# Four F blocks computed ahead instead of six, in a linear-attention and gated-FFN kernel

## The chip, the cores and the metric

The kernel runs on one core of one Trainium2 chip. TensorE (PE) multiplies matrices, VectorE (DVE), ScalarE (ACT) and GpSimd (POOL) work on elements, and SyncE (SP) issues most of the transfers. Each engine takes its own instructions strictly in the order in which they were written out; between engines only semaphores order the work. The metric is the device time of one execution in microseconds, as the median of several runs.

## The reference

```python
def reference(A_x, A_wqkv, A_w_phi, A_wo, B_x, B_w_gate, B_w_up, B_w_down):
    xn = _layernorm(A_x)
    # attention: q, k, v from xn @ wqkv, 32 heads of 18
    pq = einsum("bhsd,hdf->bhsf", q, w_phi); pk = the same of k
    phi = concatenate([softmax(p), softmax(-p)])        # of pq and of pk
    kv = einsum("bhsf,bhsd->bhfd", phi_k, v); z = phi_k.sum(s)
    s = (phi_q @ kv / (phi_q . z + 1e-6)).reshape(B, S, D) @ wo
    # gated feed-forward
    b = (silu(xn @ w_gate) * (xn @ w_up)) @ w_down
    return A_x + s * silu(b)
```

There are 2048 rows and 576 columns. The feed-forward has F = 4608 inner columns, which the kernel cuts into 36 blocks of 128: the F blocks 0 to 35.

## The kernel before

Every fp32 operand of a product is split into a high and a low part, and a product is the sum of three matmuls of parts, so that the result is accurate to fp32. The program has four sections that follow each other: the first loads and normalises x and folds the weights (until about 60 us), the second makes keys, values and their sums (to about 230 us), the third makes the queries, the attention output and its projection (to about 490 us; `q_tile`, `numer` and `project`), and the fourth is the F section, first for the half i = 0 of the rows, then for i = 1.

In the F section a unit is one F block for one half of the rows. `gate_up` computes the gate and the up product of a unit by Strassen's scheme: seven products of seven matmuls of 512 columns each, 49 in all (line 706), in the PSUM tiles `px`, `py` and `pw`. Its weights come from `gate_up_weights`, one block ahead. For i = 0 they are loaded raw into `ld` (L675), POOL forms four sums and differences (L693 to L696, the two tiles `ld` and `ts`), ACT and DVE make the high and low parts `w` (L58 and L59, the helper `split`), and SP stores them to `w_dram` (L686); for i = 1 they are loaded back from there. The products with w_down (L805, `pd`) are queued in steps of two or four units and are put between the products of the units by `fill`.

Within a unit, the order on ACT matters for what follows: L747 copies `px` to `py` after the first product, L751 and L761 apply silu, and L735 (`snap`) copies `px` out after the products with S2 and S3, on which the next product into `px` waits. On DVE, L740 adds to a snap, and L766 forms the second half of the unit's output, `ha`. L889 on POOL is the first step of the down products of an F pair: it subtracts the two halves of a unit's output.

The first EARLY blocks are not computed there. `early_weights` and `early_tile` compute them in plain form, two products of 14 matmuls of 512 columns for each of two column halves of each i: 56 matmuls for a block and a half of the rows (L92, tile `pe`). Their result goes to DRAM (`h_dram`, L123), and in the F section `stored` reads it back (L722) in place of `gate_up`. Two blocks are begun during the first sections; the others are offered to the scheduler as work of lower priority during the third section, where the scheduler puts them between the matmuls of the queries. The block EARLY - 1 is written last, just ahead of the F section, and the loads of the sums of x that Strassen needs (`operands`, L662) stand between its two halves, since they overwrite x of the half i = 1:

```python
parts = early_weights(EARLY - 1)
early_tile(EARLY - 1, 1, parts)
xo = operands(0)
early_tile(EARLY - 1, 0, parts)
ready = [gate_up_weights(*todo.pop(0))]
```

In the order of the units the early blocks stand at every fourth place, from the second place on for i = 0 and from the first on for i = 1:

```python
for f in range(EARLY):
    order.insert(4 * f + 1 - i, f)
```

At the end of the third section `project` leaves its result in PSUM, ACT copies it out to `so` (L618, two buffers) and issues the store to `s_dram` (L619). The F section's PSUM tiles take the banks of those tiles.

Of the kernel before, what the change touches and what calls it, by code (L numbers as in the profile page):

```python
# [26 lines left out]
GROUPS = [(g * GW, min(GW, D - g * GW)) for g in range((D + GW - 1) // GW)]  # L27
NG = len(GROUPS)
QS = 256
EARLY = 6  # L30
TAILS = (NF - EARLY + 3) // 4
LAG = 3
RUSH = NF - 5
# [13 lines left out]
def gated_hedgehog_kernel(ctx: ExitStack, tc, x, w_qk, w_v, w_phi, wo, w_gu, w_tail, w_down, ident_in, mask_in, out):  # L47
# [22 lines left out]
    s_dram = dram.tile([S, D], F32, name="s_dram")  # L70
    h_dram = dram.tile([2, EARLY, P, HS], F32, name="h_dram")
    x_dram = dram.tile([2, 4, P, 4, P], F32, name="x_dram")
    sum_dram = dram.tile([2, P, 4, 4, 5, P], F32, name="sum_dram")
    w_dram = dram.tile([NF - EARLY, P, 7, 4, P], F32, name="w_dram")
    t_dram = dram.tile([TAILS, 4, 3, 32, 7, P], F32, name="t_dram")
# [24 lines left out]
    def early_weights(f, behind=None):  # L100
        parts = []
        for m in (0, 2):
            raw = epool.tile([P, 2, 3, P], F32, name="raw", bufs=2)
            hi = epool.tile([P, 2, 3, P], F32R, name="wh", bufs=3)
            lo = epool.tile([P, 2, 2, P], F32R, name="wl", bufs=3)
            nc.sync.dma_start(raw, w_gu[f, :, m:m + 2])
            with tc.issue_after(behind.ins) if behind else ExitStack():
                with tc.high_priority():
                    split_rows(hi, lo, raw)
            parts.append((hi, lo))  # L110
        return parts
# [14 lines left out]
    with ExitStack() as att:  # L126
# [510 lines left out]

        for f, halves in [(1, (0,)), (0, (0,))] + [(f, (1, 0)) for f in range(2, EARLY - 1)]:
            parts = first_weights.pop() if f == 1 else early_weights(f, read[2 * NT + 1] if f == 0 else None)
# [28 lines left out]
    def gate_up_weights(i, f):  # L668

        parts, wt = {}, fw.tile([96, 7, P], F32R, name="wt", bufs=2)  # L670
        n, q = divmod(f - EARLY, 4)
        if i == 0:
# [5 lines left out]
        def ready(m, src):  # L678
            k = 1 if m == 6 else 2
            w = fw.tile([P, k, 4, P], F32R, name=f"w{k}", bufs=2 if k == 1 else 4)  # L680
            if i:
                nc.sync.dma_start(w.bitcast(F32), w_dram[f - EARLY, :, m:m + k])
            else:
# [393 lines left out]
```

## Time and profile before

| what | us |
|---|---|
| median of 3 runs | 1647.44 (1646.44 to 1647.74) |
| the profiled execution | 1646.56 |
| its span, first to last instruction | 1644.8 |
| PE busy / DVE busy / ACT busy / POOL busy | 1610.8 / 1171.6 / 719.8 / 652.2 |

The span is followed by the page; what lies outside it in the profiled execution is 1.76 us. Times in the rows are microseconds from the start of the span. A row of the timeline has the start, the length, the engine, the line, the operation, the tiles as output<-input, shapes, a count, and in brackets the idle time before it with what ended it. The chain rows have the start, the length, the engine, the tile, the line and a count. A row of the windows has, for each engine, the busy time and in brackets the number of instructions, and then the granted clock of PE (1.00 is full), the busy share of the DMA engines and GB/s.

### The profile page before, as it was taken

The page shows a single profiled execution, that of the slowest core. Times are in us where ns is not written, and L with a number is a line of the kernel's source. Part 1 is how long each engine was busy: PE and PEld are TensorE (multiplying, and loading weights), DVE is VectorE, ACT ScalarE, POOL GpSimd, SP SyncE. Part 2 cuts the span into 40 slices and gives each one's busy share as a digit, 9 for nine tenths or more (in the row PEclk, how much of TensorE's full clock was granted, in tenths as well). Part 3 has the DMA queues.
Part 4 walks back from the last instruction along what each step waited for, and adds up shares of the span by engine and source line. Part 5 has one row for each costly group of instructions (what it writes and reads, how often), then busy time and mean ns, then how long its engine had stood idle before and what let it go on. Part 6 is the DMA issues. An engine that isn't in the chain of part 4 may idle for free.

```text
span 1644.8 us, 25236 instructions
## 1 busy us (share of the span) xinstructions
PE 1610.8 (98%) x9399; PEld 1432.9 (87%) x9399; DVE 1171.6 (71%) x1729; ACT 719.8 (44%) x1399; POOL 652.2 (40%) x695
## 2 busy tenths in 40 slices
PE   6999999999999999999999999999999999999998
PEld 5899987999988788888888888888888888888887
DVE  7677768989861476887787778845566677666578
ACT  5533344454441365444444444445433333333334
POOL 3485661433210353653555454412333244133132
PEclk9999999999999999999999999999999999999999
DMA  9622243433236545545454545395545556555434
GB/s 281 208 79 78 87 132 116 119 109 119 79 121 218 199 172 179 176 172 179 174 173 172 183 166 179 131 362 164 162 128 162 168 171 213 162 179 184 140 114 173
DMA packets 121276, 266.46 MB, mean 162 GB/s; under 512 B 12770, under 2 KB 52834, under 8 KB 119362
## 3 DMA queue, kind: packets, MB, share of 16 engines
q1 hardware_dynamic: 106188, 244.49, 44.5%
q0 software_dynamic: 3072, 11.02, 2.5%
q10 hardware_dynamic: 11894, 9.35, 1.8%
q8 instruction: 74, 1.21, 0.3%
q14 instruction: 48, 0.39, 0.1%
HBM read 165.98 MB, written 98.83 MB: 161 GB/s over the span
## 4 chain that ended last, share of the span: by engine, by line
PE 91%; DVE 3%; DMA 2%; POOL 1%; issue 1%; ACT 1%; SPq 0%; ACTq 0%; POOLq 0%; DVEq 0%
PE pd L805 24%; PE px L706 24%; PE pw L706 12%; PE p L92 6%; PE pe L92 6%; PE py L706 6%; PE p L614 4%; PE po L594 2%; PE kvp L295 2%; PE vx L383 1%; PE pt L588 1%; PE vw L383 1%; DMA s_dram<-so 1%; PE tp L221 1%; DMA xn<-in_A_x 1%
## 5 line engine op out<-in xcount | busy, mean ns | idle before, releaser
L805 PEld LDWEIGHTS pd<-dw,hh 128*128 128x128 f32 x3048 | 433.0, 189 | 25.1 <-DVE dw L59 2.0
L805 PE MATMUL pd<-dw,hh 128*128 128x288 f32 x3048 | 448.8, 297 | 3.2 <-DVE dw L59 1.5
L706 PE MATMUL px<-X,w 128*128 128x512 f32 x1440 | 373.1, 393 | 1.5 <-ACT w L58 1.0
L706 PEld LDWEIGHTS px<-X,w 128*128 128x128 f32 x1440 | 261.4, 188 | 52.5 <-ACT s L735 3.3
L706 PE MATMUL pw<-X,w 128*128 128x512 f32 x720 | 185.7, 393 | 0.0
L706 PEld LDWEIGHTS pw<-X,w 128*128 128x128 f32 x720 | 134.7, 189 | 30.4 <-DVE s L740 0.3
L740 DVE TENSOR_TENSOR s<-pw,s 128x512 f32<-128x512 f32 x120 | 82.5, 688 | 98.1 <-ACT s L735 87.3
L930 DVE TENSOR_TENSOR acc<-pd,acc 128x576 f32<-128x576 f32 x128 | 96.3, 753 | 78.8 <-PE pd L805 78.7
L92 PE MATMUL pe<-X,wh 128*128 128x512 f32 (+1 forms) x460 | 145.4, 399 | 4.9 <-DVE h L122 2.0
L735 ACT COPY s<-px 128x512 f32<-128x512 f32 x120 | 70.3, 586 | 154.9 <-PE px L706 154.8
L59 DVE TENSOR_TENSOR hh<-ha,hh 128x512 fp32r<-128x512 f32 x140 | 112.5, 829 | 16.9 <-ACT hh L58 15.6
L58 ACT CAST hh<-ha 128x512 fp32r<-128x512 f32 x140 | 82.7, 619 | 95.5 <-PE pd L805 74.4
L902 POOL TENSOR_TENSOR hb<-hb 128x512 f32<-128x512 f32 x34 | 46.3, 1363 | 163.4 <-DVE hb L762 162.8
L92 PEld LDWEIGHTS pe<-X,wh 128*128 128x128 f32 (+1 forms) x460 | 84.9, 189 | 24.0 <-ACT h L119 3.0
L59 DVE TENSOR_TENSOR w<-ld,w 128x512 fp32r<-128x512 f32 (+1 forms) x90 | 76.4, 850 | 34.0 <-ACT w L58 32.9
L706 PE MATMUL px<-X,wt 96*128 96x512 f32 x240 | 94.8, 395 | 0.0
L706 PE MATMUL py<-X,w 128*128 128x512 f32 x360 | 94.4, 396 | 0.1
L915 POOL TENSOR_TENSOR ha<-ha 128x512 f32<-128x512 f32 x34 | 52.6, 1562 | 104.6 <-DVE hh L59 104.6
L889 POOL TENSOR_TENSOR h<-ha,hb 128x512 f32<-128x512 f32 x34 | 44.7, 1314 | 106.5 <-DVE ha L766 66.6
L58 ACT CAST w<-ld 128x512 fp32r<-128x512 f32 (+1 forms) x90 | 49.3, 549 | 82.9 <-POOL ld L696 52.5
L747 ACT COPY py<-px 128x512 f32<-128x512 f32 x60 | 34.3, 572 | 98.1 <-PE px L706 76.9
L693 POOL TENSOR_TENSOR ts<-ld 128x256 f32<-128x256 f32 x30 | 27.8, 927 | 120.6 <-issue 70.8
(262 smaller groups left out, 3254.3 us busy)
## 6 DMA issues: line engine op xcount, KB each, us to landing
w_dram<-w SPq DMA_DIRECT2D x87, 512.0 KB, 2.9
w<-w_dram SPq DMA_DIRECT2D x87, 512.0 KB, 4.3
wt<-t_dram SPq DMA_DIRECT2D x59, 336.0 KB, 3.7
ld<-in_B_w_gu SPq DMA_DIRECT2D x30, 512.0 KB, 4.4
X<-sum_dram SPq DMA_DIRECT2D x8, 1280.0 KB, 9.8
rt<-in_B_w_down SPq DMA_DIRECT2D x33, 288.0 KB, 3.1
rb<-in_B_w_down SPq DMA_DIRECT2D x33, 288.0 KB, 4.4
w_dram<-w SPq DMA_DIRECT2D x29, 256.0 KB, 2.0
```

The lines of the kernel that those rows point to most:

```text
L58: nc.scalar.copy(hi, src)
L59: nc.vector.tensor_sub(lo, src, hi)
L92: last = nc.tensor.matmul(ps, l, r, start=n == 0, stop=n == len(pairs) - 1)
L614: nc.tensor.matmul(ps[:, 0:HALF], a[0:w, g, jc], bw[0:w, g, n], start=k == 0, stop=k == 3 * NG - 1)
L706: nc.tensor.matmul(ps, l, r, start=first and n == 0, stop=last and n == len(mm) - 1, skip_group_check=True)
L735: nc.scalar.copy(t, ps)
L740: nc.vector.tensor_add(t, ps, t)
L805: nc.tensor.matmul(ps, l, r, start=first and n == 0 and m == 0, stop=n == len(hs) - 1 and m == 2, skip_group_check=True)
L889: sub(s, g["h"][0][0], g["h"][0][1])
L902: nc.gpsimd.tensor_add(a21, a21, g["h"][1][1])
L915: sub(a12, a12, g["h"][0][0])
L930: nc.vector.tensor_add(a2, pd[:, :, 0:HALF], a2)
```

## The change

The number of blocks that are computed ahead goes from six to four. Blocks 4 and 5 are then ordinary units of the F section, for both halves of the rows, and two places in each half's order that held a stored block hold one that is computed there.

```diff
-EARLY = 6
+EARLY = 4
```

Three things follow from it. In the third section the early blocks that are offered as filling work are 0 and 1 (in part) and 2, and the block written last is block 3 instead of 5. The arrays `w_dram`, `h_dram` and `in_B_w_tail` have two more, or two fewer, blocks; the number of tail groups stays at 8. And the scheduler writes the engines' instructions in another order. The names of tiles in the rows below carry numbers, which differ between the two programs; the last number counts the tiles.

On PE, at the end of the third section, the last rows of `project` were followed by early blocks. Before:

```order
L614 MATMUL p_4601<-WOH,ol 128x288
L92 MATMUL pe<-X_65,wh 128x512
L92 MATMUL pe<-X_65,wl 128x512
L92 MATMUL pe<-X_65,wh 128x512 x2
L92 MATMUL pe<-X_64,wh 128x512
```

Now the F section follows at once:

```order
L614 MATMUL p_4601<-WOH,ol 128x288
L744 MATMUL py<-X_60,w_5230 128x512
L706 MATMUL px<-X_60,w_5230 128x512 x6
L706 MATMUL px<-X_60,wt 128x512
L706 MATMUL pw<-X_5150,w_5239 128x512 x6
L706 MATMUL pw<-X_5150,wt 128x512
L706 MATMUL py<-X_61,w_5230 128x512 x6
```

In the program before, 214 matmuls of early blocks stand between those two rows, L614 and L744, and now none. In the third section ahead of them (from the last row of L295 to the last of L614) there were 318, and now there are 308; up to the end of the seventh of its eight projections both have 294.

On ACT at the same place, the copies of `project`, the first weights and the first copy of the F section, L747. Before:

```order
L618 COPY so_4617<-p2_4601 128x288
L58 CAST w2_5563<-ld_5560 128x2x256
L119 ACTIVATE h_5237<-pe_5221 128x512
L619 DMA s_dram_68<-so_4617 128x288
L58 CAST w1_5580<-ld_5560 128x256
L119 ACTIVATE h_5271<-pe_5255 128x512
```

Now, with the first unit and the beginning of the second Strassen unit:

```order
L618 COPY so_4617<-p2_4601 128x288
L58 CAST w2_5263<-ld_5260 128x2x256
L619 DMA s_dram_68<-so_4617 128x288
L58 CAST w1_5280<-ld_5260 128x256
L747 COPY py_5285<-px_5284 128x512
...
L58 CAST w1_5375<-ld_5355 128x256
L58 CAST w2_5367<-ts_5357 128x2x256
L751 ACTIVATE py_5380<-py_5380 128x512
L58 CAST w2_5371<-ld_5355 128x2x256
L735 COPY s_5414<-px_5379 128x512
```

L747 of the first unit now stands directly behind the casts of the second set of weights (`ld_5260`), and the first L735 of the second unit behind those of the third set (`ld_5355`).

On POOL, the sums for the third set of weights and the first steps of the down products. Before:

```order
L693 TENSOR_TENSOR ts_5657<-ld_5655 128x256
L895 TENSOR_TENSOR rt_5745<-rt_5745 128x288
L694 TENSOR_TENSOR ts_5657<-ld_5655,ts_5657 128x256
L695 TENSOR_TENSOR ld_5655<-ld_5655 128x256
L896 TENSOR_TENSOR td_5749<-rb_5747,rt_5745 128x288
L696 TENSOR_TENSOR ld_5655<-ld_5655,ts_5657 128x256
L889 TENSOR_TENSOR h_5807<-ha_5587,hb_5588 128x512
L902 TENSOR_TENSOR hb_5588<-hb_5588,hb_5651 128x512
```

Now:

```order
L889 TENSOR_TENSOR h_5507<-ha_5287,hb_5288 128x512
L693 TENSOR_TENSOR ts_5357<-ld_5355 128x256
L694 TENSOR_TENSOR ts_5357<-ld_5355,ts_5357 128x256
L695 TENSOR_TENSOR ld_5355<-ld_5355 128x256
L902 TENSOR_TENSOR hb_5288<-hb_5288,hb_5351 128x512
L696 TENSOR_TENSOR ld_5355<-ld_5355,ts_5357 128x256
```

The four operations on the third set stood ahead of L889 and L902, and now L889 stands ahead of all four and L902 ahead of the last.

## The prediction

> **What bounds the kernel now.** I read the page first, then the busy times in stretches, then the chain that ended last, and last the timeline at the two ends of the stretch that the change removes.
>
> ```profile
> PE 1610.8 (98%) x9399; PEld 1432.9 (87%) x9399; DVE 1171.6 (71%) x1729; ACT 719.8 (44%) x1399; POOL 652.2 (40%) x695
> ```
>
> TensorE (PE) is busy for 98% of the span, so a microsecond of PE work taken away or added is a microsecond of time, unless PE then waits. Whether it waits is a question of the stage:
>
> ```profile
> 300.00:350.00 50.00, 50.00 (x349) 46.06 (x348) 45.98 (x71) 21.22 (x40) 18.36 (x36) 1.00 0.36 105
> 500.00:550.00 50.00, 50.00 (x215) 40.09 (x214) 8.56 (x12) 9.03 (x17) 7.29 (x9) 1.00 0.58 209
> 550.00:600.00 50.00, 46.80 (x219) 37.89 (x219) 32.52 (x44) 25.79 (x51) 23.89 (x23) 0.97 0.55 193
> ```
>
> In the query section (first row; the columns after the length are PE, weight loads, DVE, ACT and POOL) PE has no gap, but DVE is busy for 46 of 50 us: without filling work that section would be DVE's. In the second row only PE has work: these are the early blocks that no gap of the query section had room for. In the third row, the opening of the F section, PE loses 3.2 of 50 us and its granted clock falls to 0.97.
>
> **What is removed.** The early blocks behind the attention's last matmul, and the first matmul of the F section:
>
> ```profile
> 487.96 0.29 PE L614 MATMUL p<-WOH,ol 72*128 72x288 f32 x1
> ...
> 538.98 0.40 PE L744 MATMUL py<-X,w 128*128 128x512 f32 x1
> ```
>
> ```profile
> 493.05 46.09 PE pe L92 x196
> ```
>
> The change takes two blocks, 2 x 2 x 56 = 224 matmuls of 512 columns, out of the early work. The chain row gives 46.09 / 196 = 0.2352 us for one, so 52.7 us of PE. By the order of the instructions almost all of it comes from this stretch: the 214 matmuls between the two rows go, and the query section loses 10 of 318, all in its last eighth. So the cover of the softmax stays, and I cost it at nothing up to there. Of the ten I count four as standing where PE has something else at hand and the rest as standing in waits that will now show; I take 0.3 us of gain, between 0 and 2.35 (all ten).
>
> **What is added.** Two Strassen units for each half of the rows. The price is in the chain, as the distance between the same place in two groups of four units, first with one stored block in the group, then with none:
>
> ```profile
> 714.06 4.80 PE pd L805 x36
> ...
> 770.44 4.80 PE pd L805 x36
> ...
> 912.18 4.19 PE px L706 x18
> ...
> 980.02 4.20 PE px L706 x18
> ...
> 1297.77 4.98 PE pd L805 x36
> ...
> 1354.31 4.98 PE pd L805 x36
> ...
> 1457.56 4.19 PE px L706 x18
> ...
> 1525.42 4.19 PE px L706 x18
> ```
>
> For i = 0 that is 67.84 - 56.38 = 11.46 us for one unit more, for i = 1 it is 67.86 - 56.54 = 11.32. Two of each are 45.6 us. This price holds all that the unit issues, since PE is without gaps in both kinds of group: the splits on ACT and DVE, POOL's four operations, the transfers of weights on SP's queue, and the read of the stored block that falls away. Work alone would thus give 45.6 - 52.7 = -7.1 us.
>
> **What the removed stretch hid.** Against that stands what ran beside those 50 us: the copies and stores of the last projection and two sets of weights for the F section. On ACT:
>
> ```profile
> 488.46 0.40 ACT L618 COPY so<-p 128x288 f32<-128x288 f32 x1 [2.53 <-DMA s_dram<-so]
> ...
> 491.58 0.40 ACT L618 COPY so<-p 128x288 f32<-128x288 f32 x1 [0.71 <-DMA s_dram<-so]
> ...
> 494.70 0.41 ACT L58 CAST w<-ld 128x256 fp32r<-128x256 f32 x1 [1.71 <-POOL ld L696]
> ...
> 541.02 0.57 ACT L747 COPY py<-px 128x512 f32<-128x512 f32 x1 [4.51 <-PE px L706]
> ```
>
> The last copy out of the projection's PSUM waits at 491.58 for a store, because there are two `so` buffers. The first matmul of the F section (L744) writes to the bank that this copy reads, so it can start at 491.58 + 0.40 = 491.98, when PE has been idle since 487.96 + 0.29 = 488.25: a wait of 3.7 us, where before PE had early blocks. The F section starts 538.98 - 491.98 = 47.0 us earlier, not 50.7. Next, the third product waits for L747 on ACT, which the new order puts behind the cast at 494.70; that cast waits for POOL. L747, 0.57 us long (last row), then ends at 494.70 + 0.41 + 0.57 = 495.7. PE reaches the third product after one matmul and two products; one product takes from 540.82 to 542.43, 1.61 us:
>
> ```profile
> 540.82 1.54 PE L706 MATMUL pw<-X,w 128*128 128x512 f32 x6
> 542.20 0.40 PE L706 MATMUL pw<-X,wt 96*128 96x512 f32 x1
> 542.43 1.54 PE L706 MATMUL py<-X,w 128*128 128x512 f32 x6
> ```
>
> 491.98 + 0.23 + 3.22 = 495.4, so 0.2 to 0.3 us more; I take 0.2. Bounds for the two waits together: 0.9 (only the copy of the second row, if its store lands early) and 6 (as long again as the wait of 2.53 for the first store).
>
> **The second Strassen unit.** In the new order POOL does L889 and L902, the first steps of the down products, ahead of the sums for the third set of weights; ACT casts that set ahead of the copy (L735) on which PE's product with S3 waits. L889 itself waits for the first unit's L766 on DVE. The pieces:
>
> ```profile
> 490.89 1.07 POOL L693 TENSOR_TENSOR ts<-ld 128x256 f32<-128x256 f32 x1 [2.48 <-DVE w L59]
> ...
> 493.94 0.73 POOL L696 TENSOR_TENSOR ld<-ld,ts 128x256 f32<-128x256 f32 x1
> ```
>
> ```profile
> L902 POOL TENSOR_TENSOR hb<-hb 128x512 f32<-128x512 f32 x34 | 46.3, 1363 | 163.4 <-DVE hb L762 162.8
> ...
> L889 POOL TENSOR_TENSOR h<-ha,hb 128x512 f32<-128x512 f32 x34 | 44.7, 1314 | 106.5 <-DVE ha L766 66.6
> ```
>
> ```profile
> 552.56 0.69 DVE L740 TENSOR_TENSOR s<-pw,s 128x512 f32<-128x512 f32 x1 [0.24 <-PE pw L706]
> ...
> 553.76 0.68 DVE L766 TENSOR_TENSOR ha<-py,s 128x512 f32<-128x512 f32 x1
> ```
>
> ```profile
> 557.40 0.62 ACT L58 CAST w<-ts 128x512 fp32r<-128x512 f32 x1 [1.19 <-PE py L706]
> 557.92 0.58 ACT L751 ACTIVATE py<-py 128x512 f32<-128x512 f32 x1
> ```
>
> Count from the start of the first unit's last L740. L766 ends at 1.3 us (two operations, overlapping a little); L889 at 2.6; the four POOL operations take 490.89 to 494.67, 3.8, and L902 1.4, which makes 7.8; the casts of `w1` and two `w`, the silu and L735 on ACT some 2.5 (0.4 for `w1`, then starts 0.52 apart as in the two rows, and 0.6 for the last), 10.3. PE starts the next product when L740 ends, at 0.75, and has three products and five matmuls, 26 x 0.23 = 6.0, until 6.8. So it waits 3.5; I take 3.3, since neighbours on POOL overlap a little too. Bounds: 1 (POOL's six operations at 0.73, the shortest row, which takes 2.1 off) and 4.7 (L889 and L902 half as long again).
>
> **The clock.** Three stretches of 3.41 us in the opening of before:
>
> ```profile
> 561.90:565.30 3.40, 2.86 (x13) 2.10 (x13) 0.69 (x1) 1.17 (x2) 0.00 (x0) 1.00 0.89 290
> ...
> 568.75:572.16 3.41, 1.82 (x7) 0.87 (x7) 3.41 (x4) 2.26 (x5) 2.85 (x2) 1.00 0.53 211
> 572.16:575.57 3.41, 3.41 (x14) 3.22 (x14) 3.27 (x6) 0.00 (x0) 1.24 (x2) 0.50 0.00 0
> ```
>
> After a stretch in which PE was busy 1.82 of 3.41 us, the next 3.41 us ran at half clock, a loss of 1.7 us; 2.86 of 3.40 did not do it. A gap of 3.7 us, wherever those stretches lie, leaves one with at most 1.54 us busy, and one of 3.3 us one with at most 1.76. So both gaps should be followed by half clock: I take 1.6 us for the first, since the second half of it may follow too, and 1.2 for the other, part of which lies in the wait itself. Bounds 0 and 3.4, 0 and 1.7.
>
> The Trainium skill, "TensorE: Matmul & The Clock Gate", Part 1 (the HAM clock gate), says that the clock halves after at least one idle window of about 3.4 us and that the windows run free. By that, a gap of 3.3 us could not do it and one of 3.7 us would rarely hold a whole window; the sum below would be 2.8 us smaller. The trace disagrees: its stretch was 53% busy.
>
> **The third place.** In before, the first down products had this wait for DVE's `dw`, which stood behind splits of weights:
>
> ```profile
> 571.97 0.97 PE L805 MATMUL pd<-dw,hh 128*128 128x288 f32 x3 [1.53 <-DVE dw L59]
> ```
>
> With the 1.7 us at half clock it cost 3.2. In the new order the load of the fourth set is issued one unit later than its like before, behind the stores, and POOL and ACT queue as above. I let the same 3.2 come again, net 0; bounds -3.2 (nothing left) and +3.3 (as the second unit, on top).
>
> **The sum.** -47.0 + 45.6 - 0.3 + 0.2 + 3.3 + 1.6 + 1.2 + 0 = +4.6 us against the profiled execution of 1646.56, thus 1651.2. The median of the runs shown is 0.9 higher, 1647.44; so I forecast 1652.0. The measurement can tell about 0.2%, 3.3 us, from no change; +4.6 is 0.28%, slower.
>
> **Rivals.** First, faster: the stores land early and the scheduler's other order costs nothing, so the F section opens as it did in before. Then -7.1 us of work and about 1 of waits, 1641.5. For it speaks that the wait of 3.7 hangs on a store's landing (2.53 and 0.71 waited for); against it, that those rows are the case's own and nothing in the change touches these stores. It decides when all losses of the opening beyond those of before stay under 3.8 us. 11%.
>
> Second, no change: the first wait comes, the second is hidden, since POOL gets to the third set before L889 or DVE is quicker; then 4.6 - 3.3 - 1.2 = +0.1, 1647.5. For it: DVE's and POOL's lengths in the opening vary by half. Against: both queues are in order, and L889 is ahead. 19%.
>
> Third, no change by the clock: PE's clock stays full after both gaps, as if only a wholly idle stretch of 3.41 us counted; 4.6 - 2.8 = +1.8, 1649.2. The row at 568.75 speaks against it. 12%.
>
> Fourth, slower still: the late third set repeats at the next unit, 3.3 + 1.2 more, 1656.5. For it: each load stands behind the stores of the set before; against: from there on down products lie between the units. 12%.
>
> The forecast itself has 46%, with a range of its own from 1650.8 to 1655. Slower thus has 46 + 12 = 58%, no change 19 + 12 = 31%, faster 11%. The range goes from 1646.5, with the second and third rivals in it, to 1656.5; it leaves out the faster rival and little else.
>
> **What would show it.** In the trace of after: 0.2352 per early matmul and none behind the last L614; L744 some 3.5 to 4 us after that, released by ACT's `so`; then L747 released by ACT's cast; a wait of about 3 us on L735 in the second unit; granted clocks of 0.5 after both; groups of 56.4 and 67.8 us as before, with two more of the latter kind. I am wrong if PE's gap at the handover is under 2 us, or if L889 comes after L696 in time without holding it, or if the last L614, at 487.96 in before, moves by more than 2 us.

## The result and the profile after

The change makes the kernel slower: 1656.71 us (median, 1655.6 to 1659.45) against 1647.14 (1645.95 to 1648.78) for the kernel before on the same chip, a ratio of 1.0065 with a 95% interval of 1.0055 to 1.0075. The forecast of 1652.0 us had the sign but not the size; the time lies 0.2 us beyond the end of its range. The span of the profiled execution is 1653.7 us against 1644.8, which is 8.9 more.

The first line of the page of the kernel after:

```profile
PE 1607.2 (97%) x9371; PEld 1429.6 (86%) x9371; DVE 1173.7 (71%) x1737; ACT 727.1 (44%) x1415; POOL 660.8 (40%) x703
```

PE is busy for 3.6 us less than before (1610.8) in a span that is 8.9 us longer, so it idles for 12.5 us more. The busy times in stretches show two of the places (the columns are those of the prediction's windows); a third is the handover between the sections, in the timeline below:

```profile
400.00:450.00 50.00, 47.54 (x313) 44.14 (x312) 39.35 (x61) 21.43 (x37) 13.64 (x28) 0.97 0.56 174
430.00:440.00 10.00, 8.13 (x48) 7.71 (x47) 9.07 (x13) 2.49 (x5) 0.16 (x1) 0.84 0.86 326
500.00:550.00 50.00, 42.52 (x180) 32.75 (x179) 26.03 (x34) 21.28 (x43) 23.71 (x24) 0.95 0.65 223
```

The loss at 500 to 550 is the opening of the F section, which was forecast. The loss at 400 to 450, with 2.5 us of idle PE, a lower clock and the DMA engines at 0.56, was not: it lies in the query section. The same stretch of before:

```profile
400.00:450.00 50.00, 50.00 (x347) 46.60 (x345) 43.08 (x65) 23.38 (x40) 13.63 (x28) 1.00 0.30 85
```

PE was full there, and the DMA engines moved half as much. How long the section lasts is read from the group of the first matmul of each projection (count, shortest, median and longest, then the start of the first and of the last). Before, and then after:

```profile
L614 PE MATMUL p<-WOH,oh x160: 290/297/407, 281.1 to 487.7; 126*128 126x288 f32 x128, 72*128 72x288 f32 x32
```

```profile
L614 PE MATMUL p<-WOH,oh x160: 290/297/442, 282.1 to 491.9; 126*128 126x288 f32 x128, 72*128 72x288 f32 x32
```

The section took 206.6 us and now takes 209.8, and it began 1.0 later. The handover and the opening in the timeline of PE, after:

```profile
492.14 0.29 PE L614 MATMUL p<-WOH,ol 72*128 72x288 f32 x1
495.96 0.80 PE L744 MATMUL py<-X,w 128*128 128x512 f32 x1 [3.53 <-ACT so L618]
496.56 2.77 PE L706 MATMUL px<-X,w 128*128 128x512 f32 x6
...
502.12 1.55 PE L706 MATMUL py<-X,w 128*128 128x512 f32 x6
...
522.45 2.93 PE L706 MATMUL px<-X,w 128*128 128x512 f32 x6 [2.87 <-ACT s L735]
...
525.57 0.40 PE L706 MATMUL px<-X,w 128*128 128x512 f32 x1
```

L744 waits for the last copy, the first products behind it run at half clock (2.77 us for six matmuls instead of 1.54), and the second unit waits on L735 and then runs at half clock again. From there on the chain has groups of the lengths that were expected, for i = 0 56.38 us with a stored block and 67.82 without:

```profile
565.40 4.80 PE pd L805 x36
621.78 4.80 PE pd L805 x36
...
763.52 4.20 PE px L706 x18
831.34 4.20 PE px L706 x18
```

Set beside the steps of the prediction, the profiled executions differ by:

| place | predicted | measured |
|---|---|---|
| until the first L614 | 0 | +1.0 (281.1 to 282.1) |
| query section, first to last L614 | -0.3 | +3.2 (206.6 to 209.8) |
| last L614 to L744 | -47.0 | -47.2 (51.0 to 3.8) |
| L744 to the end of the span | +51.9 | +51.9 (1105.8 to 1157.7) |
| sum | +4.6 | +8.9 |

So the whole error of the forecast lies ahead of the last L614. Of the 4.2 us there, the 1.0 ahead of the first L614 can't be told from the difference between two executions (the last section of this document has the spread); the 3.2 can, as the runs below show. What is new in that stretch are four transfers on SP's queue. Before, and then after:

```profile
517.89 0.32 SPq L662 DMA_DIRECT2D X<-sum_dram  x1
...
527.27 0.87 SPq L662 DMA_DIRECT2D X<-sum_dram  x2
```

```profile
388.11 0.33 SPq L662 DMA_DIRECT2D X<-sum_dram  x1
...
399.10 0.32 SPq L662 DMA_DIRECT2D X<-sum_dram  x1
...
427.75 4.15 SPq L662 DMA_DIRECT2D X<-sum_dram  x2
```

These are the loads of `operands`. They stand between the two halves of the block that is written last and wait for its i = 1 half, since they overwrite x: in the kernel after, all four waited on SP for matmuls of L92. With six blocks that half ran behind the last projection; with four it is filling work of the query section, and the loads went there with it. The chain of waits in the kernel after has, at the second and the last two of them, a store of `so`, and ACT's copy behind it waits for that store:

```profile
401.84 5.97 DMA s_dram<-so
...
428.55 7.07 DMA s_dram<-so
```

```profile
407.88 0.40 ACT L618 COPY so<-p 128x288 f32<-128x288 f32 x1 [1.63 <-DMA s_dram<-so]
...
435.70 0.40 ACT L618 COPY so<-p 128x288 f32<-128x288 f32 x1 [1.91 <-DMA s_dram<-so]
```

The counterpart of the second copy in the kernel before waited for PE alone, and briefly:

```profile
433.10 0.40 ACT L618 COPY so<-p 128x288 f32<-128x288 f32 x1 [0.52 <-PE p L614]
```

The sizes and landing times of these transfers (KB each, median us from issue to landing), from 380 to 480, the stores before and the loads after:

```profile
s_dram<-so ACTq DMA_DIRECT2D x14, 144.0 KB, 1.8
```

```profile
X<-sum_dram SPq DMA_DIRECT2D x4, 1280.0 KB, 8.1
```

A store whose like landed in 1.8 us in the kernel before holds its buffer for 6 to 7 us beside a load that takes 8.1.

The theory from this (A): the four loads hold up the stores, with two `so` buffers ACT waits for the stores, PE waits for PSUM that ACT has not copied out, and its clock falls behind the second gap. The rival (B): the loads and the slow stores only lie beside it, and the query section lost cover, since it has ten filling matmuls fewer.

### The profile page after: what moved, and what is told of

Read it like the earlier page. It is cut to its first block, busy times and chain, and to the rows that moved or that the text cites. A ratio compares the mean times of both kernels' runs of the same rounds, so it can differ in the third digit from the quotient of the medians.

```text
span 1653.7 us, 25210 instructions
## 1 busy us (share of the span) xinstructions
PE 1607.2 (97%) x9371; PEld 1429.6 (86%) x9371; DVE 1173.7 (71%) x1737; ACT 727.1 (44%) x1415; POOL 660.8 (40%) x703
## 2 busy tenths in 40 slices
DMA packets 122205, 270.46 MB, mean 164 GB/s; under 512 B 12802, under 2 KB 53890, under 8 KB 120290
## 4 chain that ended last, share of the span: by engine, by line
PE 87%; DMA 4%; DVE 3%; POOL 2%; issue 2%; ACT 1%; SPq 1%; ACTq 0%; POOLq 0%; DVEq 0%
PE px L706 24%; PE pd L805 24%; PE pw L706 12%; PE py L706 6%; PE p L92 6%; PE p L614 3%; PE pe L92 3%; PE kvp L295 2%; PE po L594 2%; PE vx L383 1%; DMA s_dram<-so 1%; PE pt L588 1%; PE vw L383 1%; DMA h_dram<-h 1%; DMA x_dram<-xr 1%
## 5 line engine op out<-in xcount | busy, mean ns | idle before, releaser
L706 PE MATMUL px<-X,w 128*128 128x512 f32 x1536 | 400.4, 395 | 3.5 <-ACT s L735 3.5
L706 PEld LDWEIGHTS px<-X,w 128*128 128x128 f32 x1536 | 280.7, 189 | 58.9 <-ACT s L735 7.4
L706 PE MATMUL pw<-X,w 128*128 128x512 f32 x768 | 199.3, 395 | 1.6 <-DVE s L740 1.6
L706 PEld LDWEIGHTS pw<-X,w 128*128 128x128 f32 x768 | 144.3, 190 | 34.8 <-DVE s L740 2.7
L740 DVE TENSOR_TENSOR s<-pw,s 128x512 f32<-128x512 f32 x128 | 88.1, 688 | 108.9 <-ACT s L735 96.6
L735 ACT COPY s<-px 128x512 f32<-128x512 f32 x128 | 75.0, 586 | 167.8 <-PE px L706 167.8
L59 DVE TENSOR_TENSOR hh<-ha,hh 128x512 fp32r<-128x512 f32 x140 | 107.4, 793 | 19.3 <-ACT hh L58 18.0
L902 POOL TENSOR_TENSOR hb<-hb 128x512 f32<-128x512 f32 x34 | 46.3, 1361 | 157.9 <-DVE hb L762 157.6
L889 POOL TENSOR_TENSOR h<-ha,hb 128x512 f32<-128x512 f32 x34 | 44.8, 1317 | 152.7 <-DVE ha L766 122.8
L92 PE MATMUL pe<-X,wh 128*128 128x512 f32 x300 | 96.8, 401 | 5.6 <-ACT h L119 2.6
L706 PE MATMUL px<-X,wt 96*128 96x512 f32 x256 | 101.5, 396 | 0.0
L706 PE MATMUL py<-X,w 128*128 128x512 f32 x384 | 100.0, 393 | 0.0
L747 ACT COPY py<-px 128x512 f32<-128x512 f32 x64 | 36.6, 572 | 109.3 <-PE px L706 84.0
L706 PEld LDWEIGHTS py<-X,w 128*128 128x128 f32 x384 | 68.9, 188 | 11.4
```

What stands on the lines that cost most here:

```text
L59: nc.vector.tensor_sub(lo, src, hi)
L92: last = nc.tensor.matmul(ps, l, r, start=n == 0, stop=n == len(pairs) - 1)
L706: nc.tensor.matmul(ps, l, r, start=first and n == 0, stop=last and n == len(mm) - 1, skip_group_check=True)
L735: nc.scalar.copy(t, ps)
L740: nc.vector.tensor_add(t, ps, t)
L889: sub(s, g["h"][0][0], g["h"][0][1])
```

## The experiments

**A third buffer for `so`.** In the changed kernel, and as a control in the kernel before:

```diff
-                        so = qk.tile([P, HALF], F32, name="so", bufs=2)
+                        so = qk.tile([P, HALF], F32, name="so", bufs=3)
```

> Changed kernel with three `so` buffers in place of two. Theory A (the four 1280 KB X loads, which now stand in the query section, hold up the stores of `so`; ACT's copies wait for these with two buffers, and PE waits for the copies): the copies no longer wait at 407.9, 435.7 and before the last one, so the last L614 comes back from 492.1 to 488 to 490, L744 follows it by about 1 us instead of 3.5, and the clock stays full behind it; 4 + 2.6 + 2 less, 1648 to 1650. Theory B (the query section lost cover, with ten fillers fewer and standing elsewhere, and the stores only lie in the row): the last L614 stays at 492, only the handover gets shorter, 1652.

> Kernel before with three `so` buffers, as a control. Both theories: PE has early blocks beside every wait of the copies there, so the time stays within 1 us of 1647.1; if it falls by more, the third buffer is worth something by itself and a_so3 has to be read against this run.

The changed kernel came to 1648.12 us, a ratio to before of 1.0008 (0.9999 to 1.0018); the control to 1646.1, 0.9997 (0.9988 to 1.0006). The order on PE up to the end of the projections is the same as without the third buffer; the opening of the F section differs by a few places. Windows and timeline of the changed kernel with three buffers:

```profile
400.00:450.00 50.00, 50.00 (x346) 46.75 (x345) 42.68 (x66) 22.71 (x39) 14.08 (x29) 1.00 0.56 174
```

```profile
489.68 0.50 PE L744 MATMUL py<-X,w 128*128 128x512 f32 x1 [0.49 <-ACT so L618]
...
513.39 1.66 PE L706 MATMUL px<-X,w 128*128 128x512 f32 x6 [2.69 <-ACT s L735]
```

```profile
L614 PE MATMUL p<-WOH,oh x160: 290/296/404, 282.9 to 488.6; 126*128 126x288 f32 x128, 72*128 72x288 f32 x32
```

The loads are where they were (DMA share 0.56, 174 GB/s), with the same fillers, and PE is full. The query section takes 205.7 us, 4.1 less; the handover 0.8 instead of 3.8; and what follows L744 1.9 less, with a full clock behind both waits. A store still holds up one of ACT's copies, but PE no longer waits for it:

```profile
436.93 0.40 ACT L618 COPY so<-p 128x288 f32<-128x288 f32 x1 [2.82 <-DMA s_dram<-so]
```

So the wait for the stores is what cost the time, as theory A says, and the ten missing fillers are no cause by themselves, against B. That it is the loads that make the stores slow this run doesn't show. The control shows that the third buffer is worth nothing where early blocks lie behind the projections.

**The loads later.** The four loads go out on ACT's queue, two behind the last store of the fifth projection and two behind that of the sixth:

```diff
-                        nc.scalar.dma_start(s_dram[r0:r0 + P, n], so)
+                        stores.append(nc.scalar.dma_start(s_dram[r0:r0 + P, n], so))
...
-            nc.sync.dma_start(t.bitcast(F32).rearrange("p c n -> p (c n)"),
-                              sum_dram[i, :, j].rearrange("p s c n -> p (s c n)"))
+            with ExitStack() if i else tc.issue_after(stores[19 if j < 2 else 23].ins):
+                (nc.sync if i else nc.scalar).dma_start(t.bitcast(F32).rearrange("p c n -> p (c n)"),
+                                                        sum_dram[i, :, j].rearrange("p s c n -> p (s c n)"))
```

> Changed kernel, two `so` buffers, but the four X loads of the first half are issued on ACT's queue behind the stores of the last two projections, out of the query section's middle. Theory A: the last L614 is back at 488 (+-1), the handover and the F section stay as they are, 1656.7 - 4 = 1652.5. Theory B: the last L614 stays at 492, 1656.7. If the loads come too late for the F section instead, L706 waits for X and the time goes above 1657.

1661.25 us, 1.0091 (1.0076 to 1.0106): slower than either theory had it. The windows of this run:

```profile
400.00:450.00 50.00, 50.00 (x334) 45.68 (x333) 41.47 (x65) 22.53 (x38) 13.65 (x28) 1.00 0.55 168
450.00:500.00 50.00, 42.07 (x259) 37.11 (x258) 30.60 (x48) 17.62 (x35) 5.76 (x7) 0.93 0.36 125
```

The loss at 400 to 450 is gone, but the edit also moved filling matmuls on PE. Their group from 360 to 520 (first and last start), in this run and in the kernel after:

```profile
L92 PE MATMUL pe<-X,wh x91: 389/395/477, 361.1 to 467.4; 128*128 128x512 f32 x72, 96*128 96x512 f32 x19
```

```profile
L92 PE MATMUL pe<-X,wh x90: 389/395/477, 359.8 to 481.6; 128*128 128x512 f32 x72, 96*128 96x512 f32 x18
```

The cover ends 14 us earlier, and PE idles between 460 and 490 with half clock behind it. No matmul of the F section waits for x. The query section takes 210.2 us. What follows, from the counterpart of L744 to the end, takes 1162.3 us, 4.6 more than after; where that comes from was not followed up. So this run has the first half of what A expects and, beside it, what an early end of the cover costs; for the choice between the theories it settles nothing.

**The loads smaller.** The order stays word for word on every engine, but each load brings one twentieth, and the products of the sums read that part four times over, so the result leaves out the rest of the columns:

```diff
-            nc.sync.dma_start(t.bitcast(F32).rearrange("p c n -> p (c n)"),
-                              sum_dram[i, :, j].rearrange("p s c n -> p (s c n)"))
+            w = slice(0, 5 * BT if i else BT // 4)
+            nc.sync.dma_start(t.bitcast(F32).rearrange("p c n -> p (c n)")[:, w],
+                              sum_dram[i, :, j].rearrange("p s c n -> p (s c n)")[:, w])
...
-            xo[n] = [v[:, :, c] for c in range(5)]
+            xo[n] = [v[:, :, c] if i else v[:, 0:1, 0].to_broadcast([P, 4, P]) for c in range(5)]
```

> Changed kernel with the same order on every engine, but each of the four X loads of the first half brings 64 KB in place of 1280, and the F section's products of the sums read those 128 columns four times over (their results leave out the rest). Theory A (the loads hold up the `so` stores): the copies at 407.9 and 435.7 don't wait for a store any more, the query section has no gap between 380 and 450, the last L614 stands at 488 (+-1), and the time is 1656.7 - 4 = 1652.5, with the handover's wait of 3.5 us as it was, since the X loads are over by then. Theory B (ten fillers fewer): the last L614 stays at 492 and the time at 1656.7.

1649.52 us, 1.0021 (1.0010 to 1.0032). Windows, the group of L614, the two copies that waited for a store, and PE's opening in this run:

```profile
400.00:450.00 50.00, 50.00 (x346) 46.65 (x345) 43.13 (x65) 23.58 (x40) 13.69 (x28) 1.00 0.33 93
```

```profile
L614 PE MATMUL p<-WOH,oh x160: 290/296/442, 280.5 to 486.9; 126*128 126x288 f32 x128, 72*128 72x288 f32 x32
```

```profile
405.43 0.40 ACT L618 COPY so<-p 128x288 f32<-128x288 f32 x1 [0.63 <-PE p L614]
...
431.48 0.40 ACT L618 COPY so<-p 128x288 f32<-128x288 f32 x1
```

```profile
490.37 0.80 PE L745 MATMUL py<-X,w 128*128 128x512 f32 x1 [2.52 <-ACT so L618]
...
516.79 2.92 PE L707 MATMUL px<-X,w 128*128 128x512 f32 x6 [2.87 <-ACT s L736]
```

Up to the F section nothing but the size of the loads differs, and the query section is back at 206.4 us. Neither copy waits for a store, and PE is full from 400 to 450, though all ten fillers are still missing. That is theory A alone. The opening of the F section is as it was, with the half clock behind both waits (0.80 for L744, 2.92 for six matmuls). At the handover, though, the clock was at 0.50 before the wait of 2.52 us began: the last matmuls of L614 already took 0.44 us instead of 0.29, from 485.73 on, behind a wait of 1.56.

The ratio fell by 0.44%, some 7 us, more than the 4 expected. The profiled executions differ by 6.1: 3.4 in the query section, 1.6 ahead of it, where the order is the same, and the rest behind it. Why the medians lie further apart is not shown; one reason may be that the profiled execution of the kernel after was a mild one. In two kernels that follow below, the one with matmuls in the gap and the one with POOL's new order and two buffers, the order is the same until the end of the projections. The section took 212.1 and 212.0 us in them, and the same two copies waited longer for stores: 2.10 and 2.43 us, and 1.98 and 2.76, where the kernel after had 1.63 and 1.91. From 400 to 450 PE was busy for 46.34 us in the second of them, at a granted clock of 0.93, where the kernel after had 47.54 at 0.97. The section thus costs 3.2 to 5.5 us more than before, by how long the gaps are and how much half clock follows them. In the nine kernels traced here in which the loads are small, come behind the projections, or meet a third buffer, it took 205.3 to 207.1 us.

**The clock behind the handover.** 14 matmuls that nobody needs stand in the gap:

```diff
-                                nc.tensor.matmul(ps[:, 0:HALF], a[0:w, g, jc], bw[0:w, g, n], start=k == 0,
+                                mm = nc.tensor.matmul(ps[:, 0:HALF], a[0:w, g, jc], bw[0:w, g, n], start=k == 0,
...
+                        done.append(mm)
...
+    spare = [eps.tile([P, BT], F32, name="pe") for _ in range(1)]
+    with tc.issue_after(done[-1].ins):
+        for ps in spare:
+            xw(ps, 0, 0, slice(0, BT), *parts[0], False)
```

> Changed kernel with 14 matmuls more, whose result nobody needs, put behind the last matmul of the projections: 14 x 0.235 = 3.3 us of PE work in the wait of 3.5 us for the copy. L744 stays where it is (within 0.4 us). If the half clock behind it comes from the idle stretch, the products behind L744 run at full clock and the time falls by 2 to 2.5, to about 1654.5; if it doesn't, the time stays at 1656.7.

1651.04 us, 1.0026 (1.0015 to 1.0036). PE in this run (L746 is L744 of the others, L708 is L706, L737 is L735):

```profile
498.92 0.50 PE L746 MATMUL py<-X,w 128*128 128x512 f32 x1 [0.35 <-ACT so L620]
499.25 1.53 PE L708 MATMUL px<-X,w 128*128 128x512 f32 x6
...
525.53 1.67 PE L708 MATMUL px<-X,w 128*128 128x512 f32 x6 [0.68 <-ACT s L737]
```

L746 comes 3.9 us after the last projection matmul, as before (3.8), and the six matmuls behind it take 1.53 us instead of 2.77: idle time was what halved the clock. From L746 to the third product it takes 4.24 us instead of 6.16, 1.9 less; at full clock the third product now waits 0.53 us for L747's copy, which the half clock had hidden. The ratio fell by 0.39%, some 6.4 us, which is more than this explains. In this kernel the scheduler also wrote POOL's L889 behind the sums of the third set, and the wait on L735 is 0.68 instead of 2.87, with a full clock behind it; the run made two changes, and the next pair takes up the second.

**The order on POOL.** L889, and with it the L902 that follows it, behind the third set's four sums; the other engines keep their order:

```diff
+    fourth = []
...
-            nc.gpsimd.tensor_sub(ld[:, 1], ld[:, 1], ts[:, 1])
+            fourth.append(nc.gpsimd.tensor_sub(ld[:, 1], ld[:, 1], ts[:, 1]))
...
-            sub(s, g["h"][0][0], g["h"][0][1])
+            with tc.issue_after(fourth[2].ins):
+                sub(s, g["h"][0][0], g["h"][0][1])
```

> Changed kernel with POOL's L889 put behind the four sums of the third set of weights, in place of ahead of them. If the order on POOL is what the second unit's wait of 2.87 us on L735 hangs on, that wait goes and with it the half clock behind it (1.5): 1656.7 - 4.4 = 1652.3. If the opening of the F section is short of weights or of down operands as a whole, the wait only moves to the next place, the down products' wait for `hh`, and the time stays above 1655.

> The same with three `so` buffers. By the order on POOL: 1648.1 - 2.7 (its wait there was 2.69, with no half clock behind it) = 1645.4. If the wait only moves: 1648.

With two buffers 1654.83 us, 1.0047 (1.0033 to 1.0061), between the two expectations. The wait of 2.87 us is gone, but one unit later there is this:

```profile
540.63 2.41 PE L708 MATMUL px<-X,w 128*128 128x512 f32 x6 [3.05 <-ACT s L737]
```

From the first matmul of the F section to the end it takes 1156.1 us, 1.6 less than after: the order on POOL did set the wait, and most of the gain was given back at the next set of weights, whose casts again stand ahead of the copy, with a lower clock behind it. With three buffers the time was 1645.06, 0.9993 (0.9984 to 1.0001), against 1.0008 (0.9999 to 1.0018) for three buffers alone: 2.5 us less, near what the order on POOL alone would give, but the intervals overlap and the profiled spans (1645.9 and 1645.5) don't show it. How much of this wait can be had for good stays open.

**The number of blocks, and versions on from there.**

```diff
-EARLY = 4
+EARLY = 5
```

> Five early blocks, half of the change. Work alone: half of -7.1, thus 1647.1 - 3.5 = 1643.6. 104 early matmuls (24.5 us) still lie behind the last projection, so the copies and stores are hidden and L744 doesn't wait for `so`. If the X loads still come behind the query section, its last L614 stays at 488 and what is lost is at most the second unit's wait: 1643.6 to 1646.5. If the loads come into the query section as with four blocks, 4 us are lost there: 1647.6.

> Seven early blocks, the change the other way. Work alone +3.5, thus 1650.6. The F section's opening keeps its cover and the waits of before, so nothing else should move; if before itself still lost something to a thin cover, less than 1650.6.

Five blocks came to 1643.87 us, 0.9986 (0.9977 to 0.9994); seven to 1649.33, 1.0021 (1.0012 to 1.0031), which is 3.5 us above before by the ratio, just what the work alone gives. With five the loads of x go out behind the projections again, the first two of the four from 495.18 on:

```profile
495.18 3.50 SPq L662 DMA_DIRECT2D X<-sum_dram  x2
```

```profile
521.63 1.65 PE L706 MATMUL px<-X,w 128*128 128x512 f32 x6 [0.20 <-ACT s L735]
...
536.03 1.66 PE L706 MATMUL px<-X,w 128*128 128x512 f32 x6 [0.54 <-ACT s L735]
```

The query section takes 206.1 us, no wait on L735 is over 0.6, and the granted clock is 1.00 in the stretches from 450 to 600. Half the change keeps about two thirds of its work's gain (2.3 of 3.5); the whole change loses all of it. Five blocks with the two edits:

> Five early blocks and three `so` buffers. PE waited 0.6 us for a copy in the last projection of the run with five blocks, and there are early blocks behind it: at most 0.6 less, 1643.3 to 1643.9.

> The same with POOL's L889 behind the third set's sums. With five blocks the wait on L735 was 0.54 us alone, so by the order on POOL at most that is gained, 1643 to 1644; later down operands could cost about as much.

1643.24 us, 0.9984 (0.9975 to 0.9992), and 1643.27, 0.9978 (0.9968 to 0.9989). Neither can be told from five blocks alone; all three lie 0.14 to 0.22% under the kernel before, and their intervals end below 1.

## Why the prediction was right or wrong

**The step that failed** is the one on the query section: "So the cover of the softmax stays, and I cost it at nothing up to there", with 0.3 us of gain for the ten fillers. It measured +3.2 in the profiled execution and up to +5.5 in another with the same order. The cover did stay; what was not counted was the four loads of x. They are of 1280 KB each, they lay inside the removed stretch (517.89 to 527.27), and the list of "what the removed stretch hid" named the copies, the stores and two sets of weights, but not them. The prediction looked at which instructions PE loses and not at which transfers wait for those instructions. With the loads at a twentieth, and with a third buffer, the section is back at 206.4 and 205.7 us. Its sign to look for, that the last L614 moves by more than 2 us, is what came: 4.2, of which 1.0 lies ahead of the section.

Why the stores are slow beside the loads is argued rather than shown. The Trainium skill, "DMA: Bandwidth & Descriptors", section on queues, rings and completion order, says that each DMA engine takes turns between the queues it has work for, a packet at a time. The pages of the profiles show that a row of the load is a packet: of the same 122205 packets the kernel after has 1915 of 8 KB and more, the one with the small loads 1403, and the difference of 512 is four loads of 128 rows. An estimate from both: store and load are of 128 rows each, and if a row of the store is a packet too, a store that takes turns with a load ends about when the load does. The stores ended at 407.81 and 435.62; the loads issued at 399.10 and 427.75 would land, by the median of 8.1 us, at 407.2 and 435.9, which agrees with it. No run changed the turns themselves. A load of x isn't the only thing that can hold up a store: at the handover one kept its buffer for 6.19 us, and for 5.94 with the small loads, while the first weights of the F section were being loaded.

**The handover** was right: a wait of 3.53 us for the copy, 3.7 predicted, with L744 3.8 us after the last L614 instead of 4.0; ACT's last two copies waited for stores, as they had before.

**The opening of the F section** was right as a sum, 51.9 us, but its terms were off in both directions, and that they cancel is luck:

| term | predicted | measured |
|---|---|---|
| four units more | 45.6 | 45.5 (11.44 for one at i = 0, 11.29 at i = 1) |
| half clock and L747 at the handover | 1.8 | 2.7 (L744 to the third product 6.16, before 3.45) |
| wait on L735 | 3.3 | 2.9 |
| half clock behind it | 1.2 | 1.5 (522.45 to 525.57, 3.12 for a product of 1.61) |
| third place and the rest | 0 | -0.7 (what is left) |

The second row is all half clock: the third product did not wait for L747. At the third place PE waited 0.93, 0.68 and 0.81 us for down operands, with a full clock, where before had 3.2 with its half clock. The mechanism of the wait on L735 is the one that was told; POOL and ACT in the kernel after:

```profile
514.07 1.29 POOL L889 TENSOR_TENSOR h<-ha,hb 128x512 f32<-128x512 f32 x1 [9.32 <-DVE ha L766]
...
519.22 0.73 POOL L696 TENSOR_TENSOR ld<-ld,ts 128x256 f32<-128x256 f32 x1
```

```profile
519.98 0.41 ACT L58 CAST w<-ld 128x256 fp32r<-128x256 f32 x1 [4.33 <-POOL ld L696]
...
521.83 0.57 ACT L735 COPY s<-px 128x512 f32<-128x512 f32 x1
```

L889 holds back the sums, the sums hold back the cast, and L735 stands behind the cast. What the prediction didn't see is that the shortage moves on when POOL is reordered.

**The clock.** Windows of 3.41 us, the second of each pair starting where PE goes on:

```profile
492.55:495.96 3.41, 0.00 (x0) 0.00 (x0) 1.46 (x3) 2.29 (x6) 0.67 (x2) 0.83 0.54 204
495.96:499.37 3.41, 3.40 (x8) 2.76 (x9) 1.84 (x2) 0.73 (x2) 3.04 (x4) 0.50 0.99 324
...
519.04:522.45 3.41, 0.55 (x3) 0.12 (x1) 1.61 (x3) 2.47 (x6) 0.91 (x2) 0.95 0.01 2
522.45:525.86 3.41, 3.41 (x9) 2.72 (x10) 0.20 (x1) 0.37 (x2) 0.00 (x0) 0.55 1.02 375
```

Both gaps halved the clock, as the prediction took it. The Trainium skill's "TensorE: Matmul & The Clock Gate", Part 1, asks for an idle window of about 3.4 us. The first gap could hold one; the second, of 2.87 us, could not, and the clock halved all the same. The trace decides against the rule here.

**The rivals.** Faster needed an opening like that of before; no change needed a hidden second wait, or a full clock. The rows above refute all three. The slower one came near the measured time for another reason; the late third set did not repeat in the kernel after (the next wait on L735 is 0.42 us there), though it did once POOL's order was changed.

## What to carry to other kernels

When work moves from one stage to another, list the transfers that wait for it in the program's order: they move too, and large loads beside a double-buffered output can hold up its small stores and then the engine that empties PSUM. A third output buffer, 144 KB here, kept PE free of that wait, but is worth nothing as long as filling work covers it. A price read as the distance between the same place in two groups of the running program held to 0.1 us here, while the terms at a section's border were off by up to half, and only their sum came out, by luck.

## What the runs showed that was not expected

- A store of 144 KB, whose like landed in 1.8 us in the kernel before, kept its buffer for 5.97 and 7.07 us beside loads of 1280 KB from another engine's queue.
- The clock fell to a half behind waits of 1.56 us (the kernel with the small loads) and 2.87, and to 0.60 in the 3.4 us behind one of 3.05, and stayed full behind one of 2.69 (the kernel with three buffers): the length of the wait alone does not decide it.
- With the same order ahead of it, the query section began at 280.5, 281.1 and 282.1 us in three kernels with four blocks. In the three with five, whose order there may differ, it began at 280.2, 281.9 and 284.6. It took 209.8, 212.0 and 212.1 us in three in which the loads and stores were the same. So one profiled execution fixes a place, and the length of such a section, only to about 2 us.
